# A DRAM buffer laid out like the band it is read into, its writes on another queue, taps on 128 partitions

## The chip, the cores and the metric

One core of a Trainium2 chip. The metric is the device time of one execution in microseconds, lower is better. A profiled execution gives a trace beside it: its span is the time from the first to the last instruction on the core.

## The reference, cut to what matters

A causal depthwise convolution whose seven taps are drawn per token and head from a softmax, followed by a soft mixture of experts over all tokens. All data are float32.

```python
# x: (8, 3584, 192); weight_gen: (8, 3584, 8 heads, 7 taps)
w = exp(weight_gen - max over taps);  w /= w.sum(over taps) + 1e-9
x_unf = the 7 rows of x that end at each token, split into 8 heads of 24
a = einsum('bshk,bskhg->bshg', w, x_unf).reshape(28672, 192)
logits = a @ phi                        # 192 x 32: 8 experts of 4 slots
d = softmax of logits over the tokens;  slot_input = d.T @ a
slot_out[e] = relu(slot_input[e] @ w1[e]) @ w2[e]
out = softmax of logits over the slots @ slot_out
```

## The kernel before, in words

**Tiling.** Each batch of 3584 tokens is cut into 35 groups of 104 tokens, a group into 4 blocks of 26. A block's convolution for four heads is a matmul (line 250): the stationary side is a *band*, 128 rows (32 input tokens x 4 heads) by 26 output tokens that holds the softmaxed taps on its diagonals and zeros elsewhere; the moving side is x with the heads on a block diagonal (`xbd`, rows h, h+4, ... of tile `big`, loaded by `loadx`, line 164, four DMAs each). One call of `conv(p)` does a pair of groups, 16 matmuls; the trace records each twice. There are 140 pairs. A band tile holds 14 groups, so 7 pairs; there are 20 of them (index s), in two tiles `bands[0]` and `bands[1]`, used in turn.

**How a band is made.** `loadw(s)` (line 167) brings the raw taps of 14 groups into one of two tiles `taps` (104 partitions: 26 tokens x 4 heads; 7 taps x 112 columns). Then come `tap_top` (VectorE, maximum over the seven), `tap_sub` (GpSimd), `tap_exp` (ScalarE), `tap_sum` and `tap_inv` (VectorE), `tap_mul` (GpSimd). `turn_out` (line 217, four DMAs) writes the result to one of two DRAM tiles `turned` of shape (26 tokens, 14, 4 heads, 112), of which 7 of the 14 places hold taps and 7 stay zero (`clear` writes these once, line 211). `turn_in` (line 227, four DMAs) reads it back with a row step of 4 x 13 instead of 4 x 14 places, which shifts token j by j rows and so lays the taps on diagonals. Each piece that it reads is 112 columns, 448 bytes.

**The rest of the loop.** `conv_out` copies a pair out of PSUM (ScalarE, every fourth VectorE; four PSUM tiles `cv`), `xpose` transposes it on TensorE (two tiles `pt`, copied out by ScalarE to `cm`), and per unit of 8 pairs `logits`, `top` (running maximum, tile `mq`), `newmax`, `dexp`, `dturn` (tile `dt`), `dispatch` (tile `acb`, line 361) and `rescale` keep a running softmax over tokens. Behind the loop come the experts and the output, whose writes fill the last 60 us.

**What sets the order.** Every engine and SP's DMA queue run in program order. For the opening the order is written out by hand. For the loop each step is entered by `op(engine, cost, reads, writes, ...)`; a small planner in the kernel (`model`) places the steps by these costs and due times, while TensorE's and SP's steps keep the order in which they are entered. `turn_at[s]`, called `kr`, is the slot (two pairs) in which band tile s % 2 becomes free: `loadw(s)` is entered at slot kr - 6, the tap steps at kr - 3, `turn_out` at kr - 1, `turn_in` at kr; the band is needed at slot 3.5 s, about four slots behind kr. SP issues all DMAs of the loop: x, taps, `turned` out and in, and the experts' weights (line 666).

In the opening band 0 is made in two parts: `FIRST` (32 of its 112 columns: pairs 0 and 1), then `REST`; the taps of band 1 are loaded after both.

Of the kernel before, what the change touches and what calls it, by code (L numbers as in the profile page):

```python
# [16 lines left out]
T = 26  # L17
# [7 lines left out]
PG = 14  # L25
NPS = B * NG // PG
PL = PG * 4 * 2
PT = 4 * T
ZK = 14
# [3 lines left out]
WARM = 9, 14  # L33
# [11 lines left out]
def conv_soft_moe(ctx, tc, xh, wh, phi, w1a, w1b, w2, out):  # L45
# [81 lines left out]
    one = keep.tile([128, 1], F32, name="one")  # L127
# [41 lines left out]
    def seven(op, s, l, tag, last):  # L169

        t = taps[s % NTAP][:, :, l]
        n = l.stop - l.start
        m = pa.tile([PT, 4, PL], F32, tag="seven", name=f"{tag}{s}_{l.start}", bufs=1)[:, :, 0:n]
# [8 lines left out]
    def tap_top(s, l):  # L182
        tops[s] = seven(ALU.max, s, l, "top",
                        lambda o, a, b: V.tensor_tensor(out=o, in0=a, in1=b, op=ALU.max))  # L184

    def tap_sub(s, l):
        t = taps[s % NTAP][:, :, l]
        G.tensor_tensor(out=t, in0=t, in1=tops.pop(s).to_broadcast([PT, KT, l.stop - l.start]),  # L188
                        op=ALU.subtract)
# [5 lines left out]
    def tap_sum(s, l):  # L195
        tsums[s] = seven(ALU.add, s, l, "sum",
                         lambda o, a, b: V.scalar_tensor_tensor(out=o, in0=a, scalar=EPS, in1=b,
                                                                op0=ALU.add, op1=ALU.add))
# [4 lines left out]
    def tap_mul(s, l):  # L203
        t = taps[s % NTAP][:, :, l]
        G.tensor_tensor(out=t, in0=t, in1=tsums.pop(s).to_broadcast([PT, KT, l.stop - l.start]),  # L205
                        op=ALU.mult)

    def clear(i):

        for z in range(2):  # L210
            SY.dma_start(turned[i][:, KT:].rearrange("j (z k) h l -> z j (k h) l", z=1)[0]
                         .rearrange("j (z q) l -> z j q l", z=2)[z], bands[1][0:T, 0 : ZK])

    def turn_out(s, l, by=(SY, SY, SY, SY)):

        for h in range(4):
            by[h].dma_start(turned[s % 2][:, 0:KT, h, l], taps[s % NTAP][h:PT:4, :, l])  # L217

    BANDS = ((0, 8), (2, 16), (10, 24), (18, T))

    def turn_in(s, l, by=(SY, SY, SY, SY)):

        rows = turned[s % 2].rearrange("j k h l -> (j k h) l")
        w = 4 * (ZK - 1)
        for a, (lo, hi) in enumerate(BANDS):
            at = w * lo + 32 * a
            by[a].dma_start(bands[s % 2][32 * a : 32 * a + 32, lo:hi, l],  # L227
                            rows[at : at + w * (hi - lo)]
                            .rearrange("(j w) l -> w j l", w=w)[0:32, :, l])
# [142 lines left out]
    FIRST, REST, ALL = slice(0, 32), slice(32, PL), slice(0, PL)  # L372
    both = (SY, A, SY, A)
    loadw(0, 0, 32)
    loadx(0)
    loadw(0, 32, PL)
    clear(0)
    tap_top(0, FIRST)
    tap_sub(0, FIRST)
    tap_exp(0, FIRST)  # L380
    tap_sum(0, FIRST)
    tap_inv(0, FIRST)
    tap_mul(0, FIRST)
    turn_out(0, FIRST, both)
    warm(1)
    tap_top(0, REST)
    tap_sub(0, REST)
    tap_exp(0, REST)
    tap_sum(0, REST)
    tap_inv(0, REST)  # L390
    tap_mul(0, REST)
    turn_in(0, FIRST, both)
# [511 lines left out]
```

## Time and profile before

| | |
|---|---|
| three runs | 433.82 us median (432.48 to 435.17) |
| profiled execution | 433.65 us, span 431.8 us |
| mean granted TensorE clock | 0.843 |
| TensorE matmul busy | 299.4 us (69%) |
| VectorE, ScalarE, GpSimd busy | 207.9, 170.1, 125.0 us |
| DMA, SP's queue | 68389 packets, 88.40 MB, 69.4% of 16 engines' span |
| first pair of band 1, end of the last pair | 51.91 us, 345.1 us |

Times in the trace are microseconds from the span's start. A row of the timeline gives start, duration, engine, source line, operation, tiles written and read, and in brackets how long the engine had been idle and what ended that. SPq and ACTq are the DMA issues of SP and of ScalarE: their durations are the issuing, not the transfer. A group of waits is given as total, times, longest. A busy TensorE is not TensorE at its peak, since matmuls are pipelined.

### The profile page before, as it was taken

How to read it: one execution, taken by the hardware profiler on the slowest of the kernel's cores; microseconds unless marked ns; L12 is line 12 of the kernel's file. 1: busy time of each engine (PE TensorE's matmuls, PEld its weight loads, DVE VectorE, ACT ScalarE, POOL GpSimd, SP SyncE). 2: the span in 40 equal slices, each digit the busy share in tenths (PEclk: the TensorE clock that was granted, in tenths of full speed). 3: DMA queues.
4: the chain of work that ended last, by engine and by line, in shares of the span. 5: the costliest groups of instructions: out<-in, count | busy, mean ns of one | idle time of the engine just before them, and what ended most of it. 6: DMA issues, size and time to landing. Idle time of an engine off the chain costs nothing.

```text
span 431.8 us, 15659 instructions
## 1 busy us (share of the span) xinstructions
PE 299.4 (69%) x6834; PEld 225.6 (52%) x6834; DVE 207.9 (48%) x477; ACT 170.1 (39%) x372; POOL 125.0 (29%) x104
## 2 busy tenths in 40 slices
PE   7242195796977667958797695759798979877700
PEld 6242174584755455747586474647686758222200
DVE  5522352445554616706464452534753247797500
ACT  5032051353526334525365254335465323564300
POOL 4731232322434414505352242314421036000000
PEclk9658586878999696997999689787899999999655
DMA  4282549887788387585867778488568940699996
GB/s 124 48 257 73 121 134 239 218 192 212 203 240 208 92 233 207 157 232 152 232 171 203 207 185 214 131 210 226 155 185 227 373 184 5 239 401 399 399 402 238
DMA packets 70710, 89.89 MB, mean 208 GB/s; under 512 B 52945, under 2 KB 53329, under 8 KB 70641
## 3 DMA queue, kind: packets, MB, share of 16 engines
q1 hardware_dynamic: 68389, 88.40, 69.4%
q8 instruction: 54, 0.88, 0.9%
q10 hardware_dynamic: 2252, 0.48, 0.6%
q14 instruction: 15, 0.12, 0.1%
HBM read 59.31 MB, written 29.54 MB: 206 GB/s over the span
## 4 chain that ended last, share of the span: by engine, by line
PE 30%; DMA 25%; SPq 17%; DVE 11%; ACT 4%; issue 4%; POOL 4%; ACTq 0%; DVEq 0%; POOLq 0%
DMA taps<-wh 15%; PE cv L250 11%; PE pt L268 7%; SPq L164 6%; SPq L227 4%; PE acb L361 4%; DMA turned<-taps 4%; SPq L217 3%; POOL taps L188 3%; DMA band<-turned 3%; PE ls L297 2%; DMA out<-big 2%; DVE big L802 2%; PE po L795 2%; SPq L804 2%
## 5 line engine op out<-in xcount | busy, mean ns | idle before, releaser
L250 PE MATMUL cv<-big,band 128*26 128x96 f32 x4480 | 126.5, 269 | 43.0 <-DMA band<-turned 31.5
L250 PEld LDWEIGHTS cv<-big,band 128*26 128x26 f32 x4480 | 108.3, 132 | 57.0 <-issue 37.9
L273 ACT COPY cm<-pt 128x312 f32<-128x312 f32 x140 | 53.6, 425 | 52.8 <-PE pt L268 52.6
L188 POOL TENSOR_TENSOR taps<-taps,top 104x784 f32<-104x784 f32 (+2 forms) x21 | 37.3, 1774 | 121.0 <-DVE top L184 79.2
L268 PE MATMUL pt<-ident,tm 122*128 122x122 f32 x420 | 67.1, 302 | 2.8 <-DVE tm L256 1.6
L256 ACT COPY tm<-cv 128x384 f32<-128x384 f32 x104 | 49.8, 481 | 46.0 <-PE cv L250 32.5
L268 PEld LDWEIGHTS pt<-ident,tm 122*128 122x128 f32 x420 | 49.1, 155 | 20.6 <-issue 12.8
L205 POOL TENSOR_TENSOR taps<-taps,sum 104x784 f32<-104x784 f32 (+2 forms) x21 | 37.5, 1784 | 69.7 <-DVE sum L201 52.3
L174 DVE TENSOR_TENSOR top<-taps 104x336 f32<-104x336 f32 (+2 forms) x21 | 10.3, 492 | 95.0 <-DMA taps<-wh 93.4
L193 ACT ACTIVATE taps<-taps 104x784 f32<-104x784 f32 (+2 forms) x21 | 17.4, 827 | 91.9 <-POOL taps L188 91.8
L361 PE MATMUL acb<-tm,dt 128*32 128x193 f32 x536 | 33.5, 398 | 23.5 <-DVE dt L342 23.2
L795 PE MATMUL po<-cT,so 32*128 32x468 f32 (+3 forms) x256 | 31.8, 630 | 7.2 <-DVE big L802 6.7
L361 PEld LDWEIGHTS acb<-tm,dt 128*32 128x32 f32 x536 | 19.3, 133 | 31.9 <-DVE dt L342 24.0
L297 PE MATMUL ls<-cm,phi_sb 128*32 128x208 f32 (+1 forms) x576 | 30.2, 346 | 3.9 <-ACT cm L273 2.3
L802 ACT COPY big<-po 128x936 f32<-128x936 f32 (+2 forms) x25 | 22.4, 902 | 23.1 <-PE po L795 8.3
L802 DVE COPY big<-po 128x884 f32<-128x884 f32 (+2 forms) x24 | 25.2, 1066 | 9.1 <-DMA out<-big 6.8
L256 DVE COPY tm<-cv 128x384 f32<-128x384 f32 x36 | 19.8, 549 | 16.2 <-PE cv L250 16.1
L795 PEld LDWEIGHTS po<-cT,so 32*128 32x128 f32 (+1 forms) x256 | 10.0, 168 | 28.5 <-DVE big L802 23.9
L297 PEld LDWEIGHTS ls<-cm,phi_sb 128*32 128x32 f32 x576 | 18.6, 113 | 10.2 <-ACT cm L273 3.2
L174 DVE TENSOR_TENSOR sum<-taps 104x336 f32<-104x336 f32 (+2 forms) x21 | 10.9, 519 | 23.2 <-ACT taps L193 23.2
L320 PE MATMUL acb<-mq,sel 128*32 128x5 f32 (+1 forms) x144 | 4.4, 182 | 25.3 <-DVE mq L306 25.3
L83 POOL TENSOR_TENSOR LT<-LT,rm 128x576 f32<-128x576 f32 (+1 forms) x16 | 18.1, 1132 | 12.6 <-DVE rm L81 12.3
(111 smaller groups left out, 277.3 us busy)
## 6 DMA issues: line engine op xcount, KB each, us to landing
big<-xh SPq DMA_DIRECT2D x160, 168.0 KB
out<-big SPq DMA_DIRECT2D x23, 468.0 KB
out<-big SPq DMA_DIRECT2D x24, 442.0 KB
band<-turned SPq DMA_DIRECT2D x38, 196.0 KB
big<-w SPq DMA_DIRECT2D x8, 768.0 KB
taps<-wh SPq DMA_DIRECT2D x19, 318.5 KB
turned<-taps SPq DMA_DIRECT2D x76, 79.6 KB
band<-turned SPq DMA_DIRECT2D x38, 112.0 KB
```

What stands on the lines that cost most here:

```text
L164: SY.dma_start(xbd[h:128:4, t % NXS, h], xh[t, h])
L174: V.tensor_tensor(out=m[:, 0:3], in0=t[:, 0:3], in1=t[:, 3:6], op=op)
L188: G.tensor_tensor(out=t, in0=t, in1=tops.pop(s).to_broadcast([PT, KT, l.stop - l.start]), op=ALU.subtract)
L205: G.tensor_tensor(out=t, in0=t, in1=tsums.pop(s).to_broadcast([PT, KT, l.stop - l.start]), op=ALU.mult)
L250: P.matmul(cv[32 * blk : 32 * blk + T, o : o + 4 * GW], bands[s % 2][:, :, i], xbd[:, t % NXS, :, b * GW : (b + 1) * GW], start=True, stop ...
L256: copy(tms[u % NTM][:, pr, 1 : 2 * D + 1], cvs[p % NCV][:, 0 : 2 * D])
L268: P.transpose(pt[:, i, 0:TR], tm[0:TR, pr, 1 + 128 * i : 129 + 128 * i], ident[0:TR, 0:TR])
L273: copy(cms[u][:, pr].rearrange("p i b j -> p (i b) j"), pts.pop(p).rearrange("p i (b j) -> p (i b) j", j=32)[:, :, 0:T])
L297: P.matmul(lp[32 * blk : 32 * blk + 32, 0:n, par, 0:T], phi_sb[:, 2 * par + i, :], cm[:, 0:n, 1 if i else 2 * par, blk, :], start=(i == 0) ...
L361: P.matmul(ac[32 * q : 32 * q + 32], dt[:, g, :], tm[:, g // 2, o : o + D + 1], start=(g < 4), stop=(g + 4 >= 2 * n))
L795: P.matmul(po[dst : dst + hi - lo, at, 0 : n * T], so[32 * q : 32 * q + 32, lo:hi], cT[32 * q : 32 * q + 32, g0 : g0 + n, 0:T], start=True ...
L802: (V.tensor_copy if done[1] % 2 else A.copy)(ot.rearrange("p (q c) -> p q c", c=n * T), po[:, 0 : len(qs), 0 : n * T])
```

## The change

- The tiles `turned` take the form of the band: 152 rows, of which the first 128 are the band's partitions, by 32 columns of tokens by 112. `turn_out` now writes each tap where the band has it (a step of four rows and one column per token, four rows per tap; still 448-byte pieces), and `turn_in` reads each partition in one contiguous run of 3.5 or 6.1 KB. `clear` writes the zeros of the whole form. A third, small DRAM tile holds the `FIRST` part.
- `turn_out` is issued by ScalarE in the loop, no longer by SP. `turn_in` stays on SP and is entered at slot kr + 1; the tap steps at kr - 4.
- The taps take 32 tokens x 4 heads = 128 partitions (six tokens of each 32 are padding of zeros in the input), so their load and write grow by 128/104. The scratch tile of the maximum and sum becomes a fixed one, `sev`.
- The opening is one chain: the taps of bands 0, 1 and 2 are loaded early, band 1's taps are made right behind band 0's, and several of its steps go to VectorE. The warm-up matmuls before the first convolution are 32, formerly 14, and the clearing of tiles is spread differently.
- The planner's costs and lateness figures are changed.

```diff
-    taps = [fix.tile([PT, KT, PL], F32, name=f"taps{i}") for i in range(NTAP)]
+    taps = [fix.tile([128, KT, PL], F32, name=f"taps{i}") for i in range(NTAP)]
-    turned = [dram.tile([T, ZK, 4, PL], F32, name=f"turned{i}") for i in range(2)]
+    turned = [dram.tile([ROWS, 32, n], F32, name=f"turned{i}") for i, n in ((0, PL), (1, PL), (2, 8 * NF))]
...
-    def turn_out(s, l, by=(SY, SY, SY, SY)):
+    def turn_out(s, l, by=(A,) * 4):
+        to, z = home(s, l)
+        n = to.shape[2]
+        row = 32 * n
         for h in range(4):
-            by[h].dma_start(turned[s % 2][:, 0:KT, h, l], taps[s % NTAP][h:PT:4, :, l])
+            by[h].dma_start(bass.AP(to.tensor, to[h, 0, z.start].offset,
+                                    [[4 * row + n, 32], [4 * row, KT], [1, l.stop - l.start]]),
+                            taps[s % NTAP][32 * h : 32 * h + 32, :, l])
...
-        rows = turned[s % 2].rearrange("j k h l -> (j k h) l")
-        w = 4 * (ZK - 1)
+        at, z = home(s, l)
         for a, (lo, hi) in enumerate(BANDS):
-            at = w * lo + 32 * a
-            by[a].dma_start(bands[s % 2][32 * a : 32 * a + 32, lo:hi, l],
-                            rows[at : at + w * (hi - lo)]
-                            .rearrange("(j w) l -> w j l", w=w)[0:32, :, l])
+            r = slice(32 * a, 32 * a + 32)
+            by[a].dma_start(bands[s % 2][r, lo:hi, l], at[r, lo:hi, z])
...
-    tap_costs = ((tap_top, VE, 0.95), (tap_sub, PO, 1.6), (tap_exp, AC, 0.84), (tap_sum, VE, 0.95),
-                 (tap_inv, VE, 1.0), (tap_mul, PO, 1.6))
+    tap_costs = ((tap_top, VE, 1.4), (tap_sub, PO, 1.9), (tap_exp, AC, 0.86), (tap_sum, VE, 1.4),
+                 (tap_inv, VE, 0.9), (tap_mul, PO, 1.9))
...
-            if k == max(1, kr - 3):
+            if s >= NTAP and k == max(1 + (s > NTAP), kr - 4):
                 for f, e, c in tap_costs:
-                    op(e, c, [], [("w", s % NTAP)] + ["seven"] * (f != tap_exp), f, s, ALL, due=3.0)
-            if k == max(1, kr - 1):
-                op(SP, 1.8, [("w", s % NTAP)], [("turned", s % 2)], turn_out, s, ALL, late=2.5)
-            if k == kr:
-                op(SP, 1.8, [("turned", s % 2)], [("band", s % 2)], turn_in, s, ALL, late=3.0)
+                    op(e, c, [], [("w", s % NTAP)] + ["seven"] * (f != tap_exp), f, s, ALL, due=4.0)
+                op(AC, 1.6, [("w", s % NTAP)], [("turned", s % 2)], turn_out, s, ALL, late=3.0,
+                   due=4.0)
+            if k == (kr + 1 if s > 1 else 1):
+                op(SP, 1.6, [("turned", s % 2)], [("band", s % 2)], turn_in, s, ALL, late=3.0)
```

The hand-written opening after the change, from the loads on (some memsets left out; `both` issues two of four DMAs on SP and two on ScalarE):

```python
loadw(0, FIRST), loadw(0, REST); loadx(0); clear(2, A); clear(0); loadw(1)
tap_top(0, FIRST); tap_sub(0, FIRST, V); tap_top(0, REST); tap_exp(0, FIRST); tap_sub(0, REST)
tap_sum(0, FIRST); tap_exp(0, REST); tap_inv(0, FIRST); tap_mul(0, FIRST, V); turn_out(0, FIRST, both)
tap_sum(0, REST); tap_inv(0, REST); tap_mul(0, REST, V); turn_out(0, REST, both)
loadw(2); tap_top(1, ALL); tap_sub(1, ALL); turn_in(0, FIRST); tap_exp(1, ALL); loadx(1); clear(1)
tap_sum(1, ALL); tap_inv(1, ALL); turn_in(0, REST); warm(1)
conv(0); tap_mul(1, ALL, V); turn_out(1, ALL, both); conv_out(0); loadx(2); phi
```

SP's list in the opening, before, from the load of band 1's taps (tile `taps_85`) to the read of band 1 (`band_87`):

```order
L167 DMA taps_85<-wh 104x784
L164 DMA big<-xh 32x1344 x4
L211 DMA turned_91<-band_87 26x1568 x2
L164 DMA big<-xh 32x1344 x4
L407 DMA phi_sb<-phi 128x128
L164 DMA big<-xh 32x1344 x4
L217 DMA turned_91<-taps_85 26x7x112 x4
L167 DMA taps_84<-wh 104x784
L167 DMA taps_85<-wh 104x784
L227 DMA band_87<-turned_91 32x8x112
L227 DMA band_87<-turned_91 32x14x112 x2
L227 DMA band_87<-turned_91 32x8x112
```

and now, from the clearing of band 1's DRAM tile (`turned_92`; band 1 is `band_88`):

```order
L211 DMA turned_92<-band_88 32x896
L211 DMA turned_92<-band_88 32x1568 x2
L211 DMA turned_92<-band_88 32x896
L232 DMA band_87<-turned_91 32x8x80
L232 DMA band_87<-turned_91 32x14x80 x2
L232 DMA band_87<-turned_91 32x8x80
L223 DMA turned_92<-taps_85 32x7x112 x2
L160 DMA big<-xh 32x1344 x4
L424 DMA phi_sb<-phi 128x128
L232 DMA band_88<-turned_92 32x896
L232 DMA band_88<-turned_92 32x1568 x2
L232 DMA band_88<-turned_92 32x896
```

The load of band 1's taps has moved ahead of this piece, before the first write of band 0; only one x load and phi stand between the write and the read of band 1.

SP's list in the loop, before, from one load of taps to the next:

```order
L167 DMA taps_85<-wh 104x784
L164 DMA big<-xh 32x1344 x4
L217 DMA turned_90<-taps_84 26x7x112 x4
L164 DMA big<-xh 32x1344 x4
L666 DMA w1a_sb<-w1a 128x512
L227 DMA band_86<-turned_90 32x8x112
L227 DMA band_86<-turned_90 32x14x112 x2
L227 DMA band_86<-turned_90 32x8x112
L167 DMA taps_84<-wh 104x784
```

and now:

```order
L163 DMA taps_84<-wh 128x784
L160 DMA big<-xh 32x1344 x4
L684 DMA w1a_sb<-w1a 128x512
L160 DMA big<-xh 32x1344 x4
L232 DMA band_88<-turned_92 32x896
L232 DMA band_88<-turned_92 32x1568 x2
L232 DMA band_88<-turned_92 32x896
L163 DMA taps_85<-wh 128x784
```

The four writes to `turned` are gone from SP; each load of taps still stands right behind a read of the band. ScalarE's list in the loop now holds these writes (copies to `tm` are `conv_out`, copies to `cm` the transposes' results):

```order
L259 COPY tm_95<-cv_99 128x384
L351 ACTIVATE al_1782<-nm_1446,nm_1736 128x1
L223 DMA turned_91<-taps_84 32x7x112 x4
L276 COPY cm_1659<-pt_1811 128x312
L276 COPY cm_1659<-pt_1815 128x312
L259 COPY tm_94<-cv_97 128x384
L259 COPY tm_94<-cv_98 128x384
```

Behind the four writes stand two transposes' results and the copies of the next pairs.

More of the change, by code (lines that the diff above doesn't have):

```diff
@@ L27 @@
 PL = PG * 4 * 2
-PT = 4 * T
-ZK = 14
+NF = 4
+FIRST, REST, ALL = slice(0, 8 * NF), slice(8 * NF, PL), slice(0, PL)
+ROWS = 4 * (31 + KT)
 LAST = S - GT
@@ L167, in loadw, with seven @@
         SY.dma_start(taps[s % NTAP][:, :, lo:hi], wh[s, :, :, lo:hi])
-    def seven(op, s, l, tag, last):
+    def seven(op, s, l, last):
         t = taps[s % NTAP][:, :, l]
-        n = l.stop - l.start
-        m = pa.tile([PT, 4, PL], F32, tag="seven", name=f"{tag}{s}_{l.start}", bufs=1)[:, :, 0:n]
+        m = sev[:, :, l]
         V.tensor_tensor(out=m[:, 0:3], in0=t[:, 0:3], in1=t[:, 3:6], op=op)
@@ L182, in tap_top, with tap_sub @@
     def tap_top(s, l):
-        tops[s] = seven(ALU.max, s, l, "top",
-                        lambda o, a, b: V.tensor_tensor(out=o, in0=a, in1=b, op=ALU.max))
-    def tap_sub(s, l):
+        tops[s, l.start] = seven(
+            ALU.max, s, l,
+            lambda o, a, b: V.tensor_tensor(out=o, in0=a, in1=b, op=ALU.max))
+    def tap_sub(s, l, eng=G):
         t = taps[s % NTAP][:, :, l]
-        G.tensor_tensor(out=t, in0=t, in1=tops.pop(s).to_broadcast([PT, KT, l.stop - l.start]),
-                        op=ALU.subtract)
+        eng.tensor_tensor(out=t, in0=t, op=ALU.subtract,
+                          in1=tops.pop((s, l.start)).to_broadcast([128, KT, l.stop - l.start]))
     def tap_exp(s, l):
@@ L195, in tap_sum @@
     def tap_sum(s, l):
-        tsums[s] = seven(ALU.add, s, l, "sum",
+        tsums[s] = seven(ALU.add, s, l,
                          lambda o, a, b: V.scalar_tensor_tensor(out=o, in0=a, scalar=EPS, in1=b,
@@ L370, in rescale @@
                                    op0=ALU.mult, op1=ALU.add)
-    FIRST, REST, ALL = slice(0, 32), slice(32, PL), slice(0, PL)
     both = (SY, A, SY, A)
-    loadw(0, 0, 32)
+    loadw(0, 0, FIRST.stop)
+    loadw(0, REST.start, PL)
     loadx(0)
-    loadw(0, 32, PL)
+    clear(2, A)
     clear(0)
+    loadw(1)
+    for t in cvs[0:2]:
+        A.copy(t, zero.to_broadcast([128, 512]))
     tap_top(0, FIRST)
-    tap_sub(0, FIRST)
+    tap_sub(0, FIRST, V)
+    tap_top(0, REST)
     tap_exp(0, FIRST)
+    A.copy(bands[0][:, 0:14], zero.unsqueeze(1).to_broadcast([128, 14, PL]))
+    tap_sub(0, REST)
+    G.memset(bands[0][:, 14:], 0.0)
     tap_sum(0, FIRST)
+    tap_exp(0, REST)
     tap_inv(0, FIRST)
-    tap_mul(0, FIRST)
+    tap_mul(0, FIRST, V)
     turn_out(0, FIRST, both)
[L385 to L388, printed above, removed]
     tap_sum(0, REST)
     tap_inv(0, REST)
-    tap_mul(0, REST)
-    turn_in(0, FIRST, both)
+    G.memset(xbd[:, 1, 0], 0.0)
+    tap_mul(0, REST, V)
     turn_out(0, REST, both)
-    V.memset(bands[1][:, ZK : 20], 0.0)
-    G.memset(bands[1][:, 20:], 0.0)
-    turn_in(0, REST, both)
-    for h in range(4):
-        (V.memset, G.memset)[h % 2](xbd[:, 1, h], 0.0)
-    loadw(1)
+    loadw(2)
+    tap_top(1, ALL)
+    G.memset(xbd[:, 1, 1], 0.0)
+    tap_sub(1, ALL)
+    turn_in(0, FIRST)
+    V.memset(xbd[:, 1, 2], 0.0)
+    G.memset(xbd[:, 1, 3], 0.0)
+    tap_exp(1, ALL)
     loadx(1)
     clear(1)
+    tap_sum(1, ALL)
+    tap_inv(1, ALL)
+    turn_in(0, REST)
+    for t in cvs[2:]:
+        V.memset(t, 0.0)
+    warm(1)
     conv(0)
+    tap_mul(1, ALL, V)
+    turn_out(1, ALL, both)
     conv_out(0)
```

54 lines of the change are left out of this document (28 added, 26 removed).

## The prediction

> **What bounds the kernel now.** I read the stages first, then the waits, then one turn of the loop that feeds the band. The windows show, per stretch, busy time with the number of instructions, granted clock, DMA share and GB/s:
>
> ```profile
> core 0: us, PE busy (x) PEld busy (x) DVE busy (x) ACT busy (x) POOL busy (x), PEclk, DMA share, GB/s
> 0.00:52.00 52.00, 18.69 (x286) 16.81 (x290) 20.07 (x54) 13.94 (x26) 20.80 (x32) 0.72 0.51 129
> 51.90:304.90 253.00, 191.16 (x4835) 152.49 (x4838) 124.72 (x314) 107.14 (x255) 86.96 (x56) 0.86 0.73 194
> 304.90:327.50 22.60, 22.60 (x642) 18.95 (x638) 12.39 (x29) 13.83 (x34) 7.24 (x6) 0.92 0.64 176
> 345.10:431.80 86.70, 52.38 (x710) 26.04 (x708) 45.58 (x67) 28.40 (x41) 10.01 (x11) 0.83 0.73 284
> ```
>
> and the same stretch for the convolution's line alone:
>
> ```profile
> 304.90:327.50 22.60, 12.83 (x480) 11.00 (x472) 0.92 0.64 176
> ```
>
> Up to 52 us TensorE does almost nothing; from 52 to 305 us it idles a quarter of the time; from 304.9 us, where the last tap set has been started, it never idles. A pair leaves 32 records there, so 480 records are 15 pairs: 22.6 / 15 = 1.51 us a pair, **10.5 us** for the seven pairs of one band. That is TensorE's own pace. The loop runs from the first pair of band 1 (51.9 us) to 345.1 us, 133 pairs or 19 bands: 293.2 / 19 = **15.43 us a band**. So about 5 us a band, and much of the first 52 us, is waiting. For what, the waits say (total us, times, longest):
>
> ```profile
> DVE top L174 <- DMA taps<-wh: 93.4, 18, 10.5
> ...
> PE cv L250 <- DMA band<-turned: 31.5, 3, 16.6
> ...
> PE acb L320 <- DVE mq L306: 25.3, 10, 6.9
> ...
> PE acb L361 <- DVE dt L342: 23.2, 4, 6.7
> ```
>
> All three band waits lie in the opening. In the loop TensorE waits for two small VectorE results, the running maximum (mq) and the turned exponentials (dt), and VectorE is late with both because it stands, in its fixed order, at a tap set's first maximum whose weights have not landed: 18 times, 5.2 us each. Long stops also cost clock:
>
> ```profile
> 108.57 1.48 PE L361 MATMUL acb<-tm,dt 128*32 128x193 f32 x32
> ...
> 143.96 2.80 PE L361 MATMUL acb<-tm,dt 128*32 128x193 f32 x32 [5.12 <-DVE dt L342]
> ```
>
> The same dispatch takes 1.48 us in a run of work and 2.80 us after a 5 us gap.
>
> Why are the weights late? One turn of the loop on one of the two tap buffers, from load to load:
>
> ```profile
> 106.88 0.37 SPq L167 DMA_DIRECT2D taps<-wh  x1
> ...
> 112.74 0.51 DVE L174 TENSOR_TENSOR top<-taps 104x336 f32<-104x336 f32 x1 [2.88 <-DMA taps<-wh]
> ...
> 119.51 1.86 POOL L205 TENSOR_TENSOR taps<-taps,sum 104x784 f32<-104x784 f32 x1 [3.39 <-DVE sum L201]
> ...
> 122.39 2.72 SPq L164 DMA_DIRECT2D big<-xh  x4
> 125.91 0.37 SPq L666 DMA_DIRECT2D w1a_sb<-w1a  x1
> 126.72 3.43 SPq L217 DMA_DIRECT2D turned<-taps  x4
> 130.25 2.92 SPq L164 DMA_DIRECT2D big<-xh  x4
> 133.22 0.59 SPq L666 DMA_DIRECT2D w1a_sb<-w1a  x1
> 133.92 1.89 SPq L227 DMA_DIRECT2D band<-turned  x4
> 135.91 0.37 SPq L167 DMA_DIRECT2D taps<-wh  x1
> ```
>
> Load to first maximum 5.86 us; to the end of the final multiply 8.63 (121.37); then **5.35 us** in which the finished taps wait only for SP, which is at the x loads; issue 3.43; 3.77 to the read of the band; that read 1.89; 0.1: 29.0 us for two bands. The mean loop is 2 x 15.43 = 30.9. The next load stands right behind the band's read, so this loop sets the pace.
>
> **The change, part by part.** *Writes on ScalarE's queue.* Four issues leave SP and stand among ScalarE's copies. Their price, and that of the nearest forms (min/median/max ns):
>
> ```profile
> L217 SPq DMA_DIRECT2D turned<-taps x80: 784/823/1475, 9.3 to 320.4; - x80
> L217 ACTq DMA_DIRECT2D turned<-taps x4: 807/842/1708, 9.3 to 17.0; - x4
> L211 SPq DMA_DIRECT2D turned<-band x4: 353/458/587, 5.7 to 26.1; - x4
> ```
>
> The new form (contiguous partitions, seven pieces a row) is not in the trace; it costs between 0.35 us (the clear) and 0.84 (ScalarE's own old writes). I take 0.82, since the pieces on the DRAM side stay: 3.3 us a band on ScalarE. The 5.35 us of SP's order go; about 1 us of ScalarE's order takes their place (a copy is 0.5 us, two may stand ahead). Saved 4.35 a loop, **2.2 us a band** (between 0 and 2.7). Queued behind the writes stand the copies out of PSUM, and TensorE waits for these. That in-order blocking is real here:
>
> ```profile
> 21.67 0.87 ACTq L227 DMA_DIRECT2D band<-turned  x2
> ...
> 22.64 0.48 ACT L256 COPY tm<-cv 128x384 f32<-128x384 f32 x1 [9.96 <-POOL big L405]
> ```
>
> The copy of pair 0, whose matmuls were long done, starts 0.1 us behind ScalarE's last issue. Four PSUM buffers for convolutions and two for transposes let TensorE run about 1.5 us on; of 3.3 us it loses up to 1.8, most of it inside the slack that a 12 to 13 us band leaves over 10.5. I charge **0.3 us a band** (0 to 1.8).
>
> The Trainium skill speaks against this part: its page "DMA: Bandwidth & Descriptors", section "Issuing engines are not separate DMA queues", holds that issuing from several engines saves only sequencer time, usually small beside the transfer. The 5.35 us row disagrees as far as waiting in SP's order is sequencer time too; if only the 3.43 us of issue count, they are merely moved, and the result is the second rival below.
>
> *Reads in contiguous runs.* Packets, sizes (KB each), and the window of the output stage:
>
> ```profile
> DMA packets 70710, 89.89 MB, mean 208 GB/s; under 512 B 52945, under 2 KB 53329, under 8 KB 70641
> ...
> band<-turned SPq DMA_DIRECT2D x38, 196.0 KB
> taps<-wh SPq DMA_DIRECT2D x19, 318.5 KB
> turned<-taps SPq DMA_DIRECT2D x76, 79.6 KB
> band<-turned SPq DMA_DIRECT2D x38, 112.0 KB
> ...
> 372.00:431.80 59.80, 28.63 (x236) 8.61 (x232) 30.23 (x34) 20.64 (x23) 0.00 (x0) 0.75 0.95 371
> ```
>
> In the output stage large packets move 371 / 0.95 = 391 GB/s of busy time. A band of the loop moves 194 x 15.43 = 2.99 MB in 0.73 x 15.43 = 11.3 us of DMA time. About 0.96 MB of it are 448-byte pieces (0.63 read, 0.33 written); the other 2.03 MB at 391 take 5.2 us, so the pieces take 6.1 us, 157 GB/s. The read as long runs falls from 4.0 to 1.6 us. The taps on 128 partitions add 23% to load and write: +0.2 and +0.5 us. DMA time falls to 9.6 us a band: not a bound at 12.8. The tap load queues behind that read, so it lands up to 2.4 us earlier, less its own growth; I take 1.5 a loop, **0.75 us a band** (0 to 1.2). The same page, "Why a DMA increments its semaphore by 16 and not by 1", has 104 partitions on 13 DMA engines and 128 on 16; by that the load's +0.2 vanishes and the sum falls by 0.1 us a band, some 2 us in all. No run here shows engines per transfer.
>
> *Taps on 128 partitions* keep the number of elements per partition, so I let the tap instructions cost what they cost now; a slowdown would show in every one of them. *Reads placed later* (one slot further on) and taps a slot earlier: the read now waits for nothing SP itself issues, and is needed two and a half slots, over 7 us, later; its issue (1.89) and landing (3 to 6) just fit. If the cover goes, TensorE waits 1 to 2 us at a band's start; the first two bands after the opening have least room and may.
>
> A band: 15.43 - 2.2 - 0.75 + 0.3 = **12.8 us**; with the bounds, 11.6 to 14.2 is likely, 10.5 the floor.
>
> *Opening.* The waits and SP's steps now:
>
> ```profile
> 14.78 1.37 POOL L205 TENSOR_TENSOR taps<-taps,sum 104x560 f32<-104x560 f32 x1 [2.80 <-DVE sum L201]
> ...
> 16.17 1.65 SPq L217 DMA_DIRECT2D turned<-taps  x2
> ...
> 21.64 0.81 SPq L227 DMA_DIRECT2D band<-turned  x2
> ...
> 22.98 2.45 SPq L164 DMA_DIRECT2D big<-xh  x4
> ...
> 29.49 0.58 SPq L407 DMA_DIRECT2D phi_sb<-phi  x1
> ...
> 44.19 1.89 SPq L227 DMA_DIRECT2D band<-turned  x4
> ...
> 51.91 1.50 PE L250 MATMUL cv<-big,band 128*26 128x96 f32 x32 [16.65 <-DMA band<-turned]
> ```
>
> Band 1 waits because its taps are started only after band 0 is complete. In the new order both run together, and the end is set by SP's list. The second multiply moves to VectorE and ends at about 12 us (16.15 now; I bound it by 11 and 16). From there: two writes 1.65, landing 3.8 (17.82 to 21.64), tap load 0.45, four reads 1.65, x load 2.45, four clears at 0.458, four reads 1.65, two writes 1.65, x load 2.4, phi 0.58, four reads 1.89, landing 5.8 (46.08 to 51.91): 12 + 25.8 = **38 us** for band 1's first pair instead of 51.9 (33 to 43). The first pairs come later than now, at about 21 us, behind the load and the reads, but they have 17 us until band 1 lands and need 10. The longer warm-up and the rearranged clearing lie in that same wait and cost nothing; without it, 18 more warm-up matmuls would cost about 6 us by the 7.6 us of the present 23.
>
> **Sum**, for the profiled execution (433.65 us, span 431.8, so 1.85 outside it; the median is 433.82): 38 + 19 x 12.8 + 86.7 from the last pair to the end + 1.85 = **370 us**.
>
> **The rivals.** (1) *TensorE's pace.* If the load lands before VectorE asks for it, all mq and dt waits go: 38 + 19 x 10.7 + 88.5 = 330 us. For it: the gapless stretch. Against: there no tap work is left, and the loop above still needs 24 us or more for two bands. (2) *Only the opening gains.* The new order again asks for a tap set's maximum one to three pairs after its load is issued, as now, and ScalarE's order may hold the writes as SP's did: the band stays at 15.4 and the time is 38 + 293 + 88.5 = 420 us. For it: 93.4 us of waits that came from the same kind of fixed order. (3) *Slower: the copies.* Rival 2 holds, and ScalarE's 3.3 us of writes come on top, before the copies that TensorE needs: 1.8 us a band, plus any wait for GpSimd's multiply. Then 17.2 us a band and 454 us. It decides from 16.1 us a band, that is from 0.7 us a band above today; for it speaks the copy of pair 0, against it that ScalarE is busy only 107 of 253 us.
>
> **How the numbers follow.** Forecast 0.68 (its own range 346 to 397, from 11.6 to 14.2 us a band), rival 1 0.11, rival 2 0.14, rival 3 0.07. The range takes in the forecast and rival 2: 345 to 425. One per cent, 4.3 us, is about what a measurement of this kernel tells from no change; faster than that are the forecast, rival 1 and nearly all of rival 2: 0.92; slower 0.06; the rest 0.02.
>
> **What would show it.** Band 1's first pair near 38 us; 243 us from there to the last pair; ScalarE's queue with four writes near 0.8 us each, starting within 1 us of GpSimd's multiply; load to load 25 to 26 us; VectorE's 93 us at the tap maximum about halved and TensorE's mq and dt waits from 48 us to about 20; the DMA time for the same bytes down. I am wrong if the copies on ScalarE wait behind the writes and TensorE for them, if TensorE starts to wait for the band in the loop, or if the load lands no sooner.

## The result, and the profile after

| | before | after |
|---|---|---|
| median of the runs made together | 433.77 us (432.48 to 435.17) | 379.81 us (378.68 to 381.42) |
| ratio to before | 1 | 0.8758, 95% interval 0.8713 to 0.8803 |
| profiled execution, span | 433.65, 431.8 us | 379.08, 377.1 us |
| mean granted TensorE clock | 0.843 | 0.905 |
| first pair of band 1 | 51.91 us | 37.77 us |
| a band of the loop | 15.42 us | 13.23 us |
| from the last pair to the end | 86.9 us | 87.9 us |

The forecast was 370 us (369.75 before rounding), 9.3 us too low against the profiled execution. A ratio leaves out runs that lie over 1.5% above the fastest of their kernel, so it need not be the quotient of the medians. The windows of after, cut at the first pair of band 1 and the last convolution:

```profile
core 0: us, PE busy (x) PEld busy (x) DVE busy (x) ACT busy (x) POOL busy (x), PEclk, DMA share, GB/s
0.00:37.80 37.80, 21.07 (x322) 19.67 (x323) 23.17 (x58) 12.91 (x24) 17.41 (x28) 0.82 0.81 203
37.80:289.20 251.40, 214.48 (x5842) 172.97 (x5844) 144.97 (x357) 124.73 (x306) 95.32 (x61) 0.95 0.83 245
289.20:377.10 87.90, 53.64 (x722) 26.29 (x712) 45.61 (x68) 28.69 (x42) 10.03 (x11) 0.81 0.72 281
```

The cuts come from two rows, the first convolution of band 1 in the timeline and the group of all convolutions (minimum/median/maximum ns, then the first and last start):

```profile
37.77 0.89 PE L253 MATMUL cv<-big,band 128*26 128x96 f32 x32 [1.86 <-DMA band<-turned]
```

```profile
L253 PE MATMUL cv<-big,band x4480: 243/246/371, 22.1 to 289.2; 128*26 128x96 f32 x195
```

(289.2 - 37.77) / 19 = 13.23 us a band. In the loop TensorE is busy 85% of the time at a granted clock of 0.95. Over the same part of the kernel before it was 78% at 0.87:

```profile
51.90:345.00 293.10, 228.34 (x5844) 182.75 (x5844) 142.35 (x358) 127.70 (x306) 94.19 (x61) 0.87 0.74 200
```

Of the 41.7 us that the loop lost, 27.8 are idle time of TensorE (64.8 to 36.9) and 13.9 are shorter busy time for the same work, at the higher granted clock. The waits of after:

```profile
DVE sev L169 <- DMA taps<-wh: 42.6, 16, 6.3
...
PE cv L253 <- DMA band<-turned: 13.6, 5, 4.2
...
PE acb L364 <- DVE dt L345: 8.6, 6, 4.9
PE acb L323 <- DVE mq L309: 6.2, 4, 2.8
...
ACT tm L259 <- DMA turned<-taps: 23.5, 5, 7.8
ACT cm L276 <- DMA turned<-taps: 23.3, 6, 6.0
...
ACT dd L333 <- DMA turned<-taps: 8.7, 2, 5.6
```

VectorE's wait for taps is less than half of 93.4 us, and TensorE's waits for mq and dt fell from 48.5 to 14.8. New is the last group: ScalarE idles 55.5 us in all ahead of copies and exponentials, until one of its own four writes is out. One turn of the loop on one tap buffer, to be held against the turn of 29.0 us in the prediction:

```profile
127.92 0.37 SPq L163 DMA_DIRECT2D taps<-wh  x1
...
132.61 0.51 DVE L169 TENSOR_TENSOR sev<-taps 128x336 f32<-128x336 f32 x1 [1.95 <-DMA taps<-wh]
...
140.45 1.85 POOL L201 TENSOR_TENSOR taps<-taps,sev 128x784 f32<-128x784 f32 x1 [2.40 <-DVE sev L197]
...
143.71 3.48 ACTq L223 DMA_DIRECT2D turned<-taps  x4
...
151.44 1.73 SPq L232 DMA_DIRECT2D band<-turned  x4
153.26 1.35 SPq L163 DMA_DIRECT2D taps<-wh  x1
```

Load to first maximum 4.69 us (5.86 before), to the end of the multiply 9.69 (8.63), to the first write 1.41 (5.35), the four writes 3.48 (3.43), from the last write to the read 4.25 (3.77), read and next load 1.82 (1.99): 25.3 us.

Read alone, this says that the prediction had its cause: the 5.35 us in which finished taps waited for SP are down to 1.41. The experiments say otherwise.

### The profile page after: what moved, and what is told of

Same layout as the page of the kernel before. It is cut to its first block, busy times and chain, and to the rows that moved or that the text cites. A ratio compares the mean times of both kernels' runs of the same rounds, so it can differ in the third digit from the quotient of the medians.

```text
span 377.1 us, 15741 instructions
## 1 busy us (share of the span) xinstructions
PE 289.2 (77%) x6870; PEld 218.9 (58%) x6870; DVE 213.7 (57%) x481; ACT 166.3 (44%) x370; POOL 122.8 (33%) x100
## 2 busy tenths in 40 slices
DMA packets 54596, 93.92 MB, mean 249 GB/s; under 512 B 33792, under 2 KB 34176, under 8 KB 54528
## 4 chain that ended last, share of the span: by engine, by line
PE 35%; DMA 27%; SPq 12%; DVE 9%; issue 6%; POOL 3%; ACT 2%; ACTq 0%; DVEq 0%
PE cv L253 14%; PE pt L271 7%; DMA turned<-taps 6%; DMA taps<-wh 6%; DMA big<-xh 5%; SPq L160 5%; DMA w1a_sb<-w1a 4%; PE acb L364 4%; DMA band<-turned 3%; SPq L232 3%; PE ls L300 3%; DMA out<-big 3%; DVE big L820 2%; PE po L813 2%; SPq L822 2%
## 5 line engine op out<-in xcount | busy, mean ns | idle before, releaser
L253 PE MATMUL cv<-big,band 128*26 128x96 f32 x4480 | 121.6, 259 | 29.9 <-DMA band<-turned 13.6
L253 PEld LDWEIGHTS cv<-big,band 128*26 128x26 f32 x4480 | 103.0, 129 | 44.0 <-issue 31.5
L271 PE MATMUL pt<-ident,tm 122*128 122x122 f32 x420 | 62.1, 286 | 5.3 <-issue 2.8
L201 POOL TENSOR_TENSOR taps<-taps,sev 128x784 f32<-128x784 f32 x18 | 33.7, 1872 | 74.9 <-DVE sev L197 52.2
L184 POOL TENSOR_TENSOR taps<-taps,sev 128x784 f32<-128x784 f32 (+1 forms) x20 | 36.9, 1843 | 65.2 <-DVE sev L180 31.4
L169 DVE TENSOR_TENSOR sev<-taps 128x336 f32<-128x336 f32 (+2 forms) x42 | 22.0, 524 | 52.6 <-DMA taps<-wh 42.6
L364 PE MATMUL acb<-tm,dt 128*32 128x193 f32 x536 | 27.4, 342 | 8.9 <-DVE dt L345 8.6
L300 PEld LDWEIGHTS ls<-cm,phi_sb 128*32 128x32 f32 x576 | 19.7, 113 | 11.3 <-issue 3.8
L96 POOL TENSOR_TENSOR LT<-LT,sm 128x576 f32<-128x576 f32 (+1 forms) x16 | 18.8, 1176 | 15.4 <-DVE sm L94 15.4
L189 ACT ACTIVATE taps<-taps 128x784 f32<-128x784 f32 (+2 forms) x21 | 17.6, 836 | 13.0 <-POOL taps L184 10.7
L307 DVE TENSOR_REDUCE mx<-ls 128x1 f32<-128x416 f32 (+1 forms) x18 | 10.3, 573 | 16.7 <-PE ls L300 16.7
```

What stands on the lines that cost most here:

```text
L169: V.tensor_tensor(out=m[:, 0:3], in0=t[:, 0:3], in1=t[:, 3:6], op=op)
L184: eng.tensor_tensor(out=t, in0=t, op=ALU.subtract, in1=tops.pop((s, l.start)).to_broadcast([128, KT, l.stop - l.start]))
L201: eng.tensor_tensor(out=t, in0=t, op=ALU.mult, in1=tsums.pop(s).to_broadcast([128, KT, l.stop - l.start]))
L253: P.matmul(cv[32 * blk : 32 * blk + T, o : o + 4 * GW], bands[s % 2][:, :, i], xbd[:, t % NXS, :, b * GW : (b + 1) * GW], start=True, stop ...
L271: P.transpose(pt[:, i, 0:TR], tm[0:TR, pr, 1 + 128 * i : 129 + 128 * i], ident[0:TR, 0:TR])
L300: P.matmul(lp[32 * blk : 32 * blk + 32, 0:n, par, 0:T], phi_sb[:, 2 * par + i, :], cm[:, 0:n, 1 if i else 2 * par, blk, :], start=(i == 0) ...
```

## The experiments

Each kernel was timed in three rounds beside the kernel before, whose median moved between 431.0 and 435.7 us from one group of runs to the next. So times of different groups are comparable to some 4 us, and the ratio stands with each.

**1. The four parts undone one at a time in the changed kernel.** First the queue: the writes go back to SP, two slots ahead of the read.

```diff
-                op(AC, 1.6, [("w", s % NTAP)], [("turned", s % 2)], turn_out, s, ALL, late=3.0,
-                   due=4.0)
+            if s >= NTAP and k == max(1 + (s > NTAP), kr - 1):
+                op(SP, 1.6, [("w", s % NTAP)], [("turned", s % 2)], turn_out, s, ALL, (SY,) * 4, late=3.0)
```

> The changed kernel with one part undone: in the loop the four writes of a band are issued by SP again, one slot before the band becomes free, ahead of the x loads as before; layout, contiguous reads, opening and reads at slot kr + 1 stay. Theory (the finished taps no longer wait in SP's order): the wait of about 5 us a loop comes back, a band goes from 13.3 to about 15.2 us, 405 to 420 us. Rival (the gain of the loop is from the contiguous reads and the earlier tap steps; the queue is only a change of place): 376 to 388 us.

380.57 us (378.54 to 382.66), ratio 0.8889 (0.8784 to 0.8994). The queue is worth 0.8 us by the medians and 1.3% by the ratios, whose intervals overlap: little, if anything. In this run's waits of SP's queue, ten times the writes wait for the multiply, and not the finished taps for SP:

```profile
SPq L223 <- POOL taps L201: 19.0, 10, 3.7
```

Next the runs: the rows in DRAM are padded by 16 columns, so that a read goes in pieces of 448 bytes again (81476 packets instead of 54596; the steps of the writes follow).

```diff
-    turned = [dram.tile([ROWS, 32, n], F32, ...) for i, n in ...]
+    turned = [dram.tile([ROWS, 32, n + 16], F32, ...)[:, :, 0:n] for i, n in ...]
...
```

> The changed kernel with the rows of the DRAM buffer padded by 16 columns per token, so that the reads of the band come in pieces of 448 bytes again instead of runs of 3.5 and 6.1 KB; same bytes, same order, same queues. Theory (each load of taps lands some 1.5 us later behind a slower read, 0.75 us a band): 385 to 400 us, with DMA time per band up by about 2 us. Rival 1 (the contiguous read is the main gain): 410 us or more. Rival 2 (the read's time is hidden): 378 to 382 us.

383.58 us (380.87 to 386.57), ratio 0.8961 (0.8839 to 0.9082); 13.31 us a band. That is 0.1 us a band more in the profiled execution, which was the fastest of the four, and 0.2 by the medians: between the theory and its second rival, and mostly hidden.

The opening: band 1's taps are made only after band 0 is complete, as before (the calls are written in the old order).

```diff
+    turn_in(0, FIRST, both); turn_in(0, REST, both)
+    loadw(1)
     loadw(2)
-    tap_top(1, ALL); tap_sub(1, ALL); tap_exp(1, ALL); tap_sum(1, ALL); tap_inv(1, ALL); tap_mul(1, ALL, V)
-    turn_out(1, ALL, both)
...
-            if s >= NTAP and k == max(1 + (s > NTAP), kr - 4):
+            if k == max(1 + (s > NTAP), kr - 4):
```

> The changed kernel with the opening taken apart again: the taps of band 1 are loaded and made only after both parts of band 0 have been written and read, with band 1's tap steps placed by the planner; the loop is the changed one. Theory: band 1's first pair goes from 37.8 to about 50 us and the whole by 10 to 15 us, 390 to 395 us. Rival (the later start is made up in the loop, because the following bands' taps are ready sooner): 380 to 384 us.

384.48 us (384.04 to 390.36), ratio 0.8976 (0.8871 to 0.9082), at the edge of the rival's range. The timeline has band 1's first pair back at its old place:

```profile
53.84 1.51 PE L253 MATMUL cv<-big,band 128*26 128x96 f32 x32 [16.21 <-DMA big<-xh]
```

That is 16.1 us later. Left of it at the end are 4.7 us by the medians, 5.6 between the profiled executions and 9 by the ratios: the first two bands take 11.3 and 12.2 us instead of 13.3 and 15.7, and the others give back the rest. At the first pairs of bands 2 and 3 TensorE waits 1.84 and 4.19 us for the band in the changed kernel; after the later start it does not wait for either of these bands.

The place of the reads: entered at slot kr.

```diff
-            if k == (kr + 1 if s > 1 else 1):
+            if k == (kr if s > 1 else 1):
```

> The changed kernel with the read of each band entered on SP one slot earlier, at slot kr, as before the change. Theory: SP then stands longer at a read whose writes have not landed and holds the x loads behind it, but the next load of taps also stands earlier: 378 to 390 us. Rival (the later place carries a good part of the gain, since it keeps SP from waiting): 395 us or more.

408.36 us (405.49 to 412.42), ratio 0.9505 (0.9321 to 0.9689). SP now stands at the reads, with the x loads and the next load of taps behind them. Its queue's wait in this run, and the same row of the changed kernel:

```profile
SPq L232 <- DMA turned<-taps: 96.7, 33, 8.7
```

```profile
SPq L232 <- DMA turned<-taps: 21.0, 12, 5.1
```

My reading after these four was that the order is the loop's gain. But the lists of SP quoted with the change show the read behind an x load (and at times a load of weights) and right ahead of a load of taps in both kernels. The place kr + 1 is where the reads were, since they are now entered ahead of their slot's x loads and not behind them. This run moves them to a place that neither kernel has: it prices a mistake, not the change.

**2. From the other end: the order alone in the kernel before, and one detail of form in the changed one.** In the kernel before, two steps move ahead of the x loads of their slot: the tap steps, from slot kr - 3, and the writes, which stood behind the x loads.

```diff
+            if s > 2 and k == kr - 4:
...
+            if s > 2 and k == kr - 1:
                op(SP, 1.8, [("w", s % NTAP)], [("turned", s % 2)], turn_out, s, ALL, late=2.5)
```

> The kernel before with only the places in the order changed: the tap steps are entered a slot earlier and the writes ahead of the x loads of their slot, so that SP's list has the order of the run with the writes on SP (in the kernel before the band's reads already stand right ahead of the next tap load). Layout, read pieces and opening stay as before. Theory P (the order is the loop's gain): a band falls to about 13.5 us, 385 to 400 us in all. Theory F (the form of the writes is the gain: 32 neighbouring partitions at 0.3 to 0.46 us of issue instead of every fourth partition at 0.82, on an SP that issues in 23.5 of 26.3 us): the order alone leaves 420 to 433 us.

428.66 us (423.96 to 434.76), ratio 0.9926 (0.9871 to 0.9981): the order is worth under 2%, and theory P fell.

In the run with the writes on SP, the rows 32 h + j of a tap set become 4 j + h again (the input's layout follows):

```diff
-                            taps[s % NTAP][32 * h : 32 * h + 32, :, l])
+                            taps[s % NTAP][h:128:4, :, l])
```

> The run with the writes on SP (380.6 us), but the 128 rows of a tap set in the old order (partition 4 j + h instead of 32 h + j), so that each write again takes every fourth partition; the data and everything else stay. Theory F: the issue of a write goes back to about 0.8 us, 1.5 us a band more on SP, and with it 19 x 1.5 = 28 us: 400 to 415 us. Theory P: SP has room for it, 380 to 387 us.

388.33 us (387.77 to 389.01), ratio 0.9006 (0.8944 to 0.9069): 7.8 us over the run with neighbouring rows, so theory F has its direction and a quarter of its size. The issue of a write, in this run and in the one before it:

```profile
L223 SPq DMA_DIRECT2D turned<-taps x78: 577/626/1884, 10.4 to 273.7; - x78
```

```profile
L223 SPq DMA_DIRECT2D turned<-taps x78: 303/444/1616, 10.5 to 262.7; - x78
```

Neither theory had the 48 us between 428.7 and 380.6. SP's waits in the kernel before in the changed order pointed to a circle:

```profile
SPq L164 <- PE cv L250: 33.7, 15, 5.6
```

SP stands at an x load for TensorE's convolution with the writes and the load of taps behind it, and TensorE is late for them. The same row of the run with the writes on SP:

```profile
SPq L160 <- PE cv L253: 4.3, 9, 0.8
```

In the changed kernel, which is as fast as that run, the row is 21.1 us, so SP's standing there does not by itself make the loop slow:

```profile
SPq L160 <- PE cv L253: 21.1, 16, 4.0
```

The test takes that wait away in the kernel before:

```diff
+            if t + NXS < NSG and max(1, (SGG * t + SGG - 1) // 4) + 1 == k:
+                op(SP, 1.8, [], [x_of(t)], loadx, t + NXS, late=2.2)
             if max(1, (SGG * t + SGG - 1) // 4) == k:
                 if t + NXS < NSG:
-                    op(SP, 1.8, [], [x_of(t)], loadx, t + NXS, late=2.2)
+                    pass
```

> The kernel before with one edit: the load of the x windows is entered one slot later, when TensorE has long left the buffer, so that SP no longer stands at it (36.3 us of waits for TensorE's convolution in the kernel before, 4.3 in the run with the writes on SP) with finished taps and the next tap load behind it. Theory W (the loss is a circle: TensorE late, so SP stands at the x load, so the writes and the tap load are late, so VectorE and then TensorE are late): the waits go and a band falls by 1 to 2 us, 395 to 415 us. Rival (SP's standing at x is a result of the slow loop, not a part of it): 426 to 436 us.

423.18 us (421.13 to 423.34), ratio 0.9805 (0.9741 to 0.9869). The wait is down to 4.3 us and 9 us of time came of it, less than the theory asked for. SP now stands at the reads instead, in the same run's waits:

```profile
SPq L227 <- DMA turned<-taps: 16.6, 19, 2.6
SPq L227 <- PE cv L250: 14.0, 7, 3.4
```

The circle exists, and it is small.

**3. The whole chain.** With the circle gone as an answer, the parts were undone on top of each other, down from the run with the writes on SP. The first run has both old forms, the padded rows in DRAM and the rows 4 j + h; the second has the old opening too (its edit is shown above).

```diff
+    turned = [dram.tile([ROWS, 32, n + 16], F32, ...)[:, :, 0:n] for i, n in ...]
...
+                            taps[s % NTAP][h:128:4, :, l])
```

> The run with the writes on SP with both old forms together: every fourth partition in the writes and 448-byte pieces in the reads; order, opening and 128 partitions as changed. Singly they cost 8 us (388.3) and 4 us. If they add up: 390 to 394 us, and the form is not the 48 us between the kernel before in the changed order (428.7) and this one. Theory W (past some delay the circle closes and SP stands at x again): 405 to 425 us, with over 20 us of SP's waits for TensorE at the x loads.

393.13 us (392.95 to 394.69), ratio 0.9127 (0.9069 to 0.9184): the two forms add up.

> The same with the opening in the old order too (band 1's taps after band 0): all four parts of the change undone inside the changed kernel, only 128 instead of 104 partitions, the planner's costs and the layout's row pitch left. If the four parts are the whole change: 420 to 432 us, as the kernel before in the changed order (428.7). If the parts add up as measured singly (8 + 4 + 5): 395 to 400 us, and what is left over, 28 us, belongs to the partitions, the pitch or the planner's costs.

410.87 us (407.28 to 412.23), ratio 0.9541 (0.9462 to 0.9620), between its two expectations. The opening costs 17.7 us here by the medians and 12.6 between the profiled executions, where it cost 4.7 and 5.6 on top of the fast loop. The loop gives next to nothing back: 14.00 us a band against 14.05. Some 18 us were left to the kernel before in the changed order. On top of it, 26 tap rows a head instead of 32:

```diff
-    taps = [fix.tile([128, KT, PL], F32, ...) for i in range(NTAP)]
+    taps = [fix.tile([104, KT, PL], F32, ...) for i in range(NTAP)]
...
-                            taps[s % NTAP][h:128:4, :, l])
+                            taps[s % NTAP][h:104:4, :, l])
```

> The run with all four parts undone (410.9 us), with the 104 tap rows of the kernel before in place of 128: loads, writes and tap instructions on 104 partitions, 26 rows a write. What is then left of the difference to the kernel before in the changed order (428.7 us) is the pitch of the rows in DRAM and the planner's costs. Theory N (the number of partitions: a write of 26 rows issues in 0.83 us where one of 32 takes 0.63, 0.8 us a band on SP's list, and the loads spread worse): 420 to 430 us, with writes near 0.8 us each. Rival (the pitch or the costs): 406 to 413 us, although it moves 4 MB less.

418.89 us (416.91 to 421.78), ratio 0.9647 (0.9556 to 0.9738), just below the theory's range. It is slower though it moves 3 MB less, and its writes issue as slowly as in the kernel before:

```profile
L223 SPq DMA_DIRECT2D turned<-taps x80: 784/826/1767, 15.5 to 303.9; - x80
```

The two ratios' intervals overlap, so the 8 us are likely and not certain; the rise of the issue is certain.

The chain, each row with one more part of the change. Us a band is worked out from each profiled execution as above, and one execution can lie well off the median: the one of the row "+ 128 rows" is 3.6 us below it, 0.2 us a band. If that whole difference is the loop's, the steps from the row pitch to the opening are -0.79, -0.26 and -0.22 by the medians, so a step is good to some 0.2 or 0.3 us. The row on the pitch holds whatever else the changed file has, and its opening, the new steps in the old order, is 7 us later than the real old one.

| kernel | us | ratio to before | band 1's first pair | us a band | step |
|---|---|---|---|---|---|
| before | 433.8 | 1 | 51.9 | 15.42 | |
| + order of SP and of the tap steps | 428.7 | 0.9926 | 50.3 | 15.16 | -0.26 |
| + row pitch in DRAM, planner's costs | 418.9 | 0.9647 | 57.4 | 14.48 | -0.68 |
| + 128 rows | 410.9 | 0.9541 | 54.3 | 14.00 | -0.48 |
| + opening | 393.1 | 0.9127 | 38.8 | 14.05 | +0.05 |
| + contiguous reads | 388.3 | 0.9006 | 37.8 | 13.79 | -0.26 |
| + neighbouring rows in a write | 380.6 | 0.8889 | 37.0 | 13.34 | -0.45 |
| + ScalarE's queue = after | 379.8 | 0.8758 | 37.8 | 13.23 | -0.11 |

No part carries the loop's 2.19 us. What they shorten lies in one ring. Its stages, as means over 12 or 13 turns of one buffer, worked out from the timelines (us; "writes" are the four issues). They leave out the first turns and those whose rows are merged, so their sums are not quite twice the chain's us a band:

| | load to subtract | to multiply's end | to first write | writes | to read | to load |
|---|---|---|---|---|---|---|
| before | 7.36 | 7.48 | 5.96 | 3.75 | 4.47 | 2.42 |
| order changed | 7.60 | 7.53 | 3.17 | 3.78 | 6.28 | 2.47 |
| all four parts undone, 128 rows | 7.38 | 7.82 | 1.89 | 3.05 | 5.58 | 2.48 |
| writes on SP | 7.09 | 7.82 | 1.88 | 2.22 | 5.39 | 2.29 |
| after | 6.60 | 8.54 | 0.81 | 3.40 | 4.05 | 2.30 |

The wait for SP had shrunk from 5.96 to 1.88 us with the writes still on SP. The queue then takes 1.07 off it, 1.34 off the way to the read and 0.49 off the load, and pays 1.18 more in the writes and 0.72 more in the tap steps, one of which is on ScalarE too.

**4. Two versions that go further.** Does the way from load to load set the pace? The changed kernel gets a third tap buffer in a part of `w1b_sb` that is filled late.

```diff
-    NTM, NCV, NTAP = 2, 4, 2
+    NTM, NCV, NTAP = 2, 4, 3
...
-            if s > NTAP and k == max(1, kr - 6):
+            if s >= NTAP and k == max(1, kr - 8):
```

> The changed kernel with a third tap buffer (in a part of the expert weights' buffer that is filled late), each load entered two slots earlier. Theory (the way from a load to the next load of the same buffer, 26 us for two bands, sets the pace): VectorE's 42.6 us of waits for taps mostly go, a band comes to 11.5 to 12.5 us, 357 to 370 us in all. Rival (the pace is set by the whole of SP's list and by the copies, not by the loads): 375 to 384 us.

374.97 us (373.06 to 377.60), ratio 0.8700 (0.8620 to 0.8780). VectorE's wait for taps falls from 42.6 us to 17.4, in two rows, since the third buffer has its own:

```profile
DVE sev L170 <- DMA taps<-wh: 13.2, 7, 5.0
...
DVE sev L170 <- DMA w1b_sb<-wh: 4.2, 3, 2.0
```

A band falls by 0.11 us only in the profiled execution, and by at most 0.25 if all that the median gained is the loop's. So VectorE's largest wait does not set the pace of the changed loop, and the theory fell.

And the copies held behind the writes: the four writes are entered as four steps, between which copies may stand.

```diff
...
-                op(AC, 1.6, [("w", s % NTAP)], [("turned", s % 2)], turn_out, s, ALL, late=3.0,
-                   due=4.0)
+                for h in range(4):
+                    op(AC, 0.4, [("w", s % NTAP)], [("turned", s % 2, h)], turn_one, s, h,
+                       late=3.0, due=4.0 + 0.8 * h)
...
```

> The changed kernel with the four writes of a band entered as four steps 0.8 us apart on ScalarE instead of one after the other, so that copies out of PSUM can stand between them. Theory (the copies held behind a group of writes, 23 us each for the two kinds, make TensorE late): 370 to 377 us. Rival (they lie in slack, or the waits come from the transfers that are eight back and stay): 378 to 384 us.

373.10 us (370.94 to 375.58), ratio 0.8672 (0.8577 to 0.8766), 12.89 us a band: the time that the theory forecast. ScalarE's waits that end with one of its own writes are down from 55.5 us to 19.9:

```profile
ACT tm L268 <- DMA turned<-taps: 11.1, 2, 6.9
...
ACT cm L285 <- DMA turned<-taps: 8.8, 2, 5.0
```

The theory's mechanism is less clear. Waits that end with the landing of an x load, at copies that need no x, are longer than in the changed kernel (first its row, then that of this run):

```profile
ACT cm L276 <- DMA big<-xh: 8.0, 2, 5.7
```

```profile
ACT cm L285 <- DMA big<-xh: 15.6, 4, 5.1
```

And the window of this loop gives TensorE 35.8 us of idle time against 36.9 in the changed kernel, while its busy time fell by 5.3 us at a clock of 0.98:

```profile
36.80:281.80 245.00, 209.21 (x5840) 168.63 (x5844) 145.28 (x361) 124.97 (x308) 94.70 (x61) 0.98 0.85 252
```

So that the held copies made TensorE late is not shown.

Both versions beat both kernels: no run of theirs is as slow as the fastest of the changed kernel, though the intervals of the ratios overlap. The two together were not tried.

## Why the prediction was right, and where only its total was

**Opening: right.** 38 us forecast, 37.77 measured. SP's list set it: the multiply of band 1's taps ended at 22.67 us, and their write left SP at 27.04. The order carries it: the chain's row with the opening moves band 1 by 15.5 us. That the number is hit so closely is luck, since single terms were off by over 1 us each way: the multiply of band 0 ended at 13.1 us and not at 12, and from the read of band 1 to its first pair it took 6.3 us and not 7.7. The opening's worth at the end is another matter: 17.7 us by the medians when the loop behind it is slow, 4.7 when it is fast. I counted a start that comes 14 us earlier as 14 us.

**The band: 12.8 forecast, 13.23 measured; 8 of the 9.3 us missed.** The sum came close by luck, on terms that were wrong:

- *The writes' queue, -2.2:* the failed step. It took the whole wait of the finished taps for an effect of the queue. The wait went as foreseen (5.96 to 0.81 in the mean), but most of it goes with the writes still on SP; the queue itself is worth 0.1 us a band, 0.3 by the ratios. The section of "DMA: Bandwidth & Descriptors" in the Trainium skill that I weighed against this part, on issuing engines, is borne out: 380.6 us from one queue, 379.8 from two. I had set the 5.35 us row against it, and a row that tells for whom an engine waits does not tell that another queue is the remedy.
- *The tap load behind a shorter read, -0.75:* 0.26 us in the chain and 0.1 to 0.2 singly. I took every microsecond of VectorE's wait for one of the loop; the third buffer, which took most of that wait away, moved a band by 0.11 to 0.25. The read's saving in DMA time was too large as well. I priced it with the output stage's 391 GB/s, 2.4 us of DMA time a band, and had DMA time fall from 11.3 to 9.6. It fell to 11.0 (0.83 x 251.4 / 19), and the run with short reads has 11.5 (0.86 x 253.0 / 19), so long reads save 0.5:

```profile
38.60:291.60 253.00, 211.38 (x5841) 170.17 (x5844) 144.78 (x357) 124.00 (x306) 94.77 (x61) 0.97 0.86 243
```

- *Copies held on ScalarE, +0.3:* about the right size by a wrong way. Splitting the writes takes 0.34 us a band off, whatever the mechanism. I priced it by an issue of 0.82 us each, for "the pieces on the DRAM side stay". The issue is 0.32 us:

```profile
L223 ACTq DMA_DIRECT2D turned<-taps x78: 309/319/1398, 10.5 to 261.5; - x78
```

and what holds ScalarE is a wait between the four: a group of them takes up to 5.9 us. The timeline has it in one place, with the copy that stands behind it:

```profile
65.07 4.90 ACTq L223 DMA_DIRECT2D turned<-taps  x4
70.01 0.48 ACT L259 COPY tm<-cv 128x384 f32<-128x384 f32 x1 [7.81 <-DMA turned<-taps]
```

- *Charged at nothing:* the 128 rows (0.48, or 0.26 by the medians), the neighbouring rows of a write (0.45, hidden in the 0.82), and the pitch with the planner's costs (0.68, or 0.79). These make up two thirds to three quarters of the loop's gain. The tap instructions themselves cost what they cost, as I had it: the multiply is 1.85 us here and was 1.86.
- *Reads a slot later, nothing:* right, since their place in SP's list is the old one.

**The tail and the time outside the span** were 87.9 and 2.0 us for 86.7 and 1.85.

**What I asked the profile to show.** Load to load 25 to 26 us: yes. VectorE's 93 us halved, TensorE's 48 us down: yes, further than I said. Writes near 0.8 us each: no, 0.32, with waits between them. 243 us from band 1's first pair to the last pair: 251.4. The DMA time for the same bytes is down a little: 270 GB/s of busy time in the loop before, 295 after (200 / 0.74 and 245 / 0.83). "The first two bands have least room": yes, 13.3 and 15.7 us. TensorE waiting for the band in the loop was to prove me wrong. It does so three times for 7.6 us in all (two of the five waits above, with 6.0 us, end with band 1's first pair or before it), too little to decide.

**The rivals.** *Only the opening gains* (420 us) fell: with the new opening, both old forms and the writes on SP the kernel takes 393.1 us at 14.05 a band. *The copies* came in the small form that the sum had. *TensorE's pace* is still 2.7 us a band away.

What stays open: which of the row pitch and the planner's costs gives the 0.68 us, the largest step of the chain, and whether the parts would be worth the same in another order. The opening was not (4.7 or 17.7 us by the medians), and the contiguous reads may not be (0.1 to 0.2 or 0.26). A wait that I left out is nearly as long as VectorE's: ScalarE, in its order, stands at a tap set's exponential for GpSimd's subtraction. Before and after:

```profile
ACT taps L193 <- POOL taps L188: 91.8, 16, 13.8
```

```profile
ACT taps L189 <- POOL taps L184: 10.7, 8, 7.6
```

TensorE's own waits for ScalarE's copies are small in both, 3.4 and 4.5 us, but no run moved this wait alone.

## What to carry to other kernels

A wait that vanishes after a change has not been shown to come from the part that was aimed at it: put that part alone back, and then build the chain from both ends until the steps meet. In a ring whose queue issues three quarters of the time (SP here, 222 of the loop's 293 us before), small prices such as the issue of one DMA can add up to more than the one large wait is worth, so price the new form of every instruction that stays. And a gain at the start of a loop is worth in full only if the loop behind it could not have made the delay good.

## What the runs showed of the hardware

The time to issue a DMA goes with the form of its source rows in SBUF, for the same pieces of 448 bytes in DRAM: 0.30 us at least for 32 neighbouring partitions, 0.58 for 32 partitions that lie four apart, 0.78 for 26 of them. So the write with fewer rows takes longest to issue, though its data land no later: by the landings in the traces 3.2 us after the start of the issue with 26 rows and 3.7 with 32 (medians of the runs with 104 and 128 rows). "DMA: Bandwidth & Descriptors" in the Trainium skill, section "Why a DMA increments its semaphore by 16 and not by 1", tells counts of partitions that spread over 16 DMA engines from others. The traces do show a difference there: in the kernel before each load of taps and each write leaves 14 updates on its completion semaphore, in the changed one 16. By that rule alone I had 0.1 us a band for the 128 rows, and the chain has 0.3 to 0.5.

The DMAs of this program take turns on eight completion semaphores, whichever queue they are in, so a write on ScalarE also waits for the DMA that used its semaphore before, which is often SP's. The group of 4.90 us above, write by write:

```profile
65.07 0.31 ACTq L223 DMA_DIRECT2D turned<-taps  x1
```

```profile
66.50 0.32 ACTq L223 DMA_DIRECT2D turned<-taps  x1
```

```profile
68.52 0.31 ACTq L223 DMA_DIRECT2D turned<-taps  x1
```

```profile
69.66 0.31 ACTq L223 DMA_DIRECT2D turned<-taps  x1
```

The earlier DMAs of these four semaphores are two reads of the band and two x loads on SP, issued 3.4 to 4.5 us before they land, and by the semaphores' updates in the trace they land at 64.98, 66.48, 68.50 and 69.64 us. Each write starts within 0.1 us of that. Of the loop's 72 writes, 38 start so. A second queue is therefore not free of the first here. No run took this wait alone away, so what it costs the loop is not shown.
